# Retention, ELU and max-out in one kernel: the loads and the order of its first eight chunks

## The chip, the cores and the metric

The kernel runs on one core of a Trainium2 chip. The metric is the device time of one execution in microseconds (us), the median over several executions. TensorE (PE in the profile) multiplies matrices, VectorE (DVE), ScalarE (ACT) and GpSimd (POOL) work elementwise, and SyncE (SP) issues most of the DMAs.

## What is computed

The reference has three layers over 4 batches of 768 tokens (3072 rows of 512).

```
state = gamma * state + outer(k_t, v_t)          # 8 heads of 64, per batch
y_t   = scale * q_t @ state
x     = y as 3072 x 512
h     = x @ w_in;  g = h if h > 0 else exp(h) - 1
x2    = g @ w_out                                 # 512 -> 2048 -> 512
h2    = max(x2 @ w1, x2 @ w2, x2 @ w3)            # 512 -> 768
out   = h2 @ moe2_w_out                           # 768 -> 512
```

The weights of the second and third layer come as 64-bit floats and are converted on the chip to a high and a low 32-bit part.

## The kernel before

**Chunks.** The recurrence is taken in 24 chunks of 128 tokens, six to a batch. A chunk `c` is one SBUF tile `x` of 128 partitions by 4 head pairs by 4 slots of 128: slot 0 is q and slot 1 is k, both with the head dimension on the partitions (first head of a pair on partitions 0 to 63, second on 64 to 127), slots 2 and 3 are k and v by token. The first eight chunks (`early`, `EARLY` = 8) read from `qkv0`, whose row of 640 floats holds two blocks of 128 for q (the first head's in the first, for partitions 0 to 63; the second head's in the second, for partitions 64 to 127), then k, k by token and v by token, 128 each. The others read from `qkv`.

**Work of a chunk.** `load` (lines 78 to 109) issues its DMAs on SP. `prep` (113 to 143) multiplies q by the decays `qdec_sb` into `qd` (line 130; left out for the first chunk of a batch) and k by token by `cols_sb` into `kd` (line 136, eight ScalarE instructions; left out for the last chunk of a batch). `scores` (145 to 154) multiplies k and q on TensorE, `mask` (156 to 169) multiplies the two results by the constants `dmask_sb` on VectorE. `mix` (194 to 217) multiplies the old state by `qd` (line 205) and the values by the masked scores (209), and ScalarE copies the sum to `xh`, the high part of the layer's input; `update` (173 to 192) makes the new state; `rest` (219) makes the low part `xl`. `begin` (531) is `scores`, `prep`, `mask`; `finish` (540) is `mix` with `update` between its matmuls and its copy. `junk(k)` (526) runs k matmuls on zeros.

**Weights.** `load_half(n)` (234) loads a half tile of weights, 512 KB in rows of 4096 bytes, into one of two staging buffers (`raw`); `cv_bits`, `cv_rest`, `cv_high` and `cv_low` (274 to 309) convert it on VectorE and ScalarE; `cv_high(n)` issues the load of half n + 2, into the buffer that half n leaves. Halves 0 and 1 serve the first `h1` and `o1` (331 and 359, the two matmul groups of the second layer, 12 matmuls of 128x512 each), halves 2 and 3 the next.

**Order.** SP, PE, DVE and ACT each run in the order in which the program text names their instructions. Each waits at its own next instruction, and nothing overtakes. The first part is written out by hand (lines 500 to 600); after it a loop runs `h1` and `o1` over blocks of 512 tokens. SP's order in the first part: chunks 0, 1, 2, half 0, chunk 3, half 1, chunks 4 to 7, then half 2, which `cv_high(0)` issues. An early chunk takes four DMAs: q of the first heads (line 98, 64 partitions, 128 KB), q of the second heads (98, 64 partitions, 128 KB), k (100, 128 partitions, 256 KB), k and v by token (106, 128 partitions, 512 KB). Each contiguous run is 512 bytes in the first three and 1024 bytes in the last. The constants `cols`, `dmask` (512 KB) and `qdec` (256 KB) are issued from ScalarE's queue. From chunk 8 on a chunk takes four DMAs of 64 partitions (98, runs of 512 bytes) and one of 128 partitions (106).

Of the kernel before, what the change touches and what calls it, by code (L numbers as in the profile page):

```python
# [15 lines left out]
B, H, S, D = 4, 8, 768, 64  # L16
P = 128
# [23 lines left out]
def kernel(ctx: ExitStack, tc: tile.TileContext, qkv0, qkv, wa, wb, dmask, qdec, cols, out):  # L41


    nc = tc.nc
# [6 lines left out]
    ps_acc = ctx.enter_context(tc.tile_pool(name="ps_acc", bufs=4, space=bass.MemoryType.PSUM))  # L51
# [9 lines left out]
    dmask_sb = const.tile([P, H, P], F32, name="dmask_sb")  # L61
    qdec_sb = const.tile([P, NPAIR, P], F32, name="qdec_sb")
# [7 lines left out]
    def f32(ap):  # L70
        return ap.bitcast(F32)
# [6 lines left out]
    def load(c, part=None):  # L78


        if c >= NCHUNK:
            return

        early = c < EARLY
        src = qkv0 if early else qkv
        if part != 1:
            if c in raw_t:
                return
            if c < EARLY + 3:
                x = wpool.tile([P, NPAIR, 4, P], F32, tag="w", name="x")  # L90
            else:
                x = ld.tile([P, NPAIR, 4, P], F32, tag="r", name="x")
            raw_t[c] = x
            for r in range(2):
                h = slice(r * D, (r + 1) * D)
                for s in range(1 if early else 2):
                    cc = slice(s * 2 * P + r * P, s * 2 * P + (r + 1) * P)
                    nc.sync.dma_start(out=x[h, :, s, :], in_=src[c, :, h, cc].rearrange("p d t -> d p t"))
            if early:
                nc.sync.dma_start(  # L100
                    out=x[:, :, 1, :], in_=src[c, :, :, 2 * P:3 * P].rearrange("p t n -> t p n")
                )
        if part != 0:
            x = raw_t[c]
            o = 3 * P if early else 4 * P
            nc.sync.dma_start(
                out=x[:, :, 2:4, :].rearrange("t p s n -> t p (s n)"),
                in_=src[c, :, :, o:].rearrange("p t n -> t p n"),
            )
# [3 lines left out]
    def prep(c):  # L113

        if c >= NCHUNK:
            return
        x = raw_t[c]
        early = c < EARLY
        pool = nc.vector if early else nc.gpsimd
        if c < EARLY + CB and c % 2:  # L120
            if c in (1, EARLY + 1):
                spare[:] = [wpool.tile([P, 4, NPAIR, P], F32, tag="w", name="spare")]
            sp = spare[0]
            qd, kd, a = sp[:, 0], sp[:, 1].rearrange("t p (r d) -> t p r d", r=2), sp[:, 2:4]
        else:
            qd = at.tile([P, NPAIR, P], F32, tag="qd", name="qd") if c % NCH != 0 else None
            kd = at.tile([P, NPAIR, 2, D], F32, tag="kd", name="kd") if c % NCH != NCH - 1 else None
            a = None
        if c % NCH != 0:
            pool.tensor_tensor(out=qd, in0=x[:, :, 0, :], in1=qdec_sb, op=ALU.mult)  # L130
        kt = x[:, :, 2, :].rearrange("t p (r d) -> t p r d", r=2)
        if c % NCH == NCH - 1:
            pass
        elif early:
            for h in range(H):
                nc.scalar.activation(kd[:, h // 2, h % 2], kt[:, h // 2, h % 2], ACTF.Copy, scale=cols_sb[:, h:h + 1])
        else:
            pool.tensor_tensor(
                out=kd, in0=kt,
                in1=cols_sb[:, 0:H].rearrange("t (p r) -> t p r", r=2).unsqueeze(3).to_broadcast([P, NPAIR, 2, D]),  # L140
                op=ALU.mult,
            )
        st_t[c] = (qd, kd, a)

    def scores(c, pool, tag):

        if c >= NCHUNK:
            return
        x = raw_t[c]
        sc = sc_t[c] = [pool.tile([P, NPAIR, P], F32, tag=tag, name="sc") for _ in range(2)]  # L150
        for p in range(NPAIR):
            for r in range(2):
                h = slice(r * D, (r + 1) * D)
                nc.tensor.matmul(sc[r][:, p, :], x[h, p, 1, :], x[h, p, 0, :], start=p == 0, stop=p == NPAIR - 1)  # L154

    def mask(c):
        if c >= NCHUNK:
            return
        sc = sc_t.pop(c)
        a = st_t[c][2]  # L160
        if a is None:
            a = at.tile([P, 2, NPAIR, P], F32, tag="a", name="a")
        else:
            a = a.rearrange("t r p i -> t r p i")
        for r in range(2):
            nc.vector.tensor_tensor(
                out=a[:, r], in0=sc[r], in1=dmask_sb.rearrange("j (p r) i -> j r p i", r=2)[:, r], op=ALU.mult
            )
        a_t[c] = a
# [49 lines left out]
    def rest(c):  # L219
        b, t0 = divmod(c * P, BLK)  # L220
        xh, xl = x_t[b]
        nc.vector.tensor_tensor(
            out=xl[:, :, t0:t0 + P], in0=xo_t.pop(c), in1=f32(xh[:, :, t0:t0 + P]), op=ALU.subtract
        )
# [49 lines left out]
    def cv_bits(n):  # L274
        if n >= len(keys):
            return
        t = dpool.tile([P, 512], I32, tag="t", name="t")
        m = dpool.tile([P, 512], F32, tag="m", name="m")
        tmp[n] = (t, m)
        nc.vector.tensor_scalar(  # L280
            out=t, in0=half[n][:, :, 1], scalar1=0x7FFFFE00, scalar2=None, op0=ALU.bitwise_and
        )
        nc.scalar.activation(t, t, ACTF.Relu, scale=8.0, bias=-896.0 * 2 ** 23)  # L283

    def cv_rest(n):
        if n >= len(keys):
            return
        m = tmp[n][1]
        lo, hi = half[n][:, :, 0].bitcast(U32), half[n][:, :, 1]
        nc.vector.tensor_scalar(out=m.bitcast(I32), in0=hi, scalar1=0x1FF, scalar2=None, op0=ALU.bitwise_and)  # L290
        nc.vector.scalar_tensor_tensor(  # L291
            out=m, in0=lo, scalar=2.0 ** -32, in1=m.bitcast(I32), op0=ALU.mult, op1=ALU.add
        )

    def cv_high(n):
        to[n] = place(n)
        t = tmp[n][0]
        nc.vector.scalar_tensor_tensor(  # L298
            out=t, in0=half[n][:, :, 1], scalar=-0x80000000, in1=t, op0=ALU.bitwise_and, op1=ALU.bitwise_or
        )  # L300
        nc.scalar.copy(to[n][:, 0], f32(t))  # L301
        load_half(n + NSTAGE)
# [200 lines left out]
    warm = dpool.tile([P, 1], F32, tag="m", name="warm")  # L503
    nc.vector.memset(warm, 0.0)
    nc.scalar.dma_start(out=cols_sb, in_=cols)
    nc.scalar.dma_start(out=dmask_sb, in_=dmask)
    nc.scalar.activation(warm, warm, ACTF.Exp)
    nc.scalar.dma_start(out=qdec_sb, in_=qdec)
    load(0)
    load(1)  # L510
    load(2)
    load_half(0)
    load(3)
# [12 lines left out]
    def junk(k):  # L526
        o = ps_h.tile([P, BLK], F32, tag="h", name="junk")
        for i in range(k):
            nc.tensor.matmul(o, zero[:, 0:P], zero, start=i == 0, stop=i == k - 1)

    def begin(c, pool=ps_h, tag="h"):
        scores(c, pool, tag)
        prep(c)
        mask(c)
# [5 lines left out]
    def finish(c):  # L540
        mix(c, ps_h, "h", update)
# [5 lines left out]
    finish(0)  # L547
    rest(0)
    junk(4)
    begin(2, ps_acc, "acc")  # L550
    finish(1)
    rest(1)
    cv_bits(0)
    begin(3, ps_acc, "acc")
    finish(2)
    rest(2)
    cv_rest(0)
    cv_high(0)
    finish(3)
# [4 lines left out]
    begin(4, ps_h, "h")  # L564
    h1(0, 0, [(cv_high, 1)])
    prep(5)
    finish(4)
    cv_low(1)
    scores(5, ps_h, "h")
    mask(5)  # L570
    rest(4)
    prep(6)
    o1(0, 0, 0, 2)
    cv_bits(2)
# [25 lines left out]
    n = 5  # L600
# [178 lines left out]
    for i, (b, f, f0, f1) in enumerate(seq):  # L779
# [8 lines left out]
        c = EARLY  # L788
# [94 lines left out]
    for v, (s, j) in enumerate(visits):  # L883
# [3 lines left out]
        if 2 <= v < 2 + KF2:  # L887
            f = v - 2
            t = ring.tile([P, 2, 512], F32R, tag=f"w{f % 2}", name="w")
# [87 lines left out]
```

## Time and profile before

| | us |
|---|---|
| median of 3 executions (1004.82 to 1005.65) | 1004.98 |
| the profiled execution | 1005.29 |
| its span, first to last instruction | 1003.5 |
| PE busy | 984.8 (98%) |
| DVE busy | 690.7 (69%) |
| ACT busy | 352.9 (35%) |
| POOL busy | 35.9 (4%) |

Busy time is that of instructions of the engine; waits and the issuing of DMAs don't count. PE's is modelled from pipelined matmuls and counts junk matmuls too. The granted TensorE clock is 1.000 of full speed over the whole span. In the DMA columns a share over 1 means that packets overlap in an engine.

### The profile page before, as it was taken

Reading aid. Unit: us, or ns where it says so; the run is one execution under the profiler, and the core shown is the slowest. Engines: PE = TensorE matmul, PEld = TensorE weight load, DVE = VectorE, ACT = ScalarE, POOL = GpSimd, SP = SyncE. Lnnn points to the kernel's source line nnn. Section 1 sums busy time; section 2 is a strip of 40 time slices with the busy share of each in tenths; the row PEclk is TensorE's granted clock in tenths of the full one; section 3 lists DMA queues with packets and bytes.
Section 4 is the critical chain, followed back from the end, with each engine's and each line's share of the span. In section 5 each row is a group of like instructions: output and inputs, shape, how many; then the busy total and the mean of one; then the engine's idle time right before and its main releaser. Section 6 shows DMA issues by size and latency. Waiting matters only on the chain.

```text
span 1003.5 us, 14377 instructions
## 1 busy us (share of the span) xinstructions
PE 984.8 (98%) x5684; PEld 848.0 (85%) x5685; DVE 690.7 (69%) x1190; ACT 352.9 (35%) x630; POOL 35.9 (4%) x31
## 2 busy tenths in 40 slices
PE   7989999999999999999999999999999999999998
PEld 5777888777888888888888788999899989989996
DVE  4889989975576776677776743688658827864771
ACT  4546555422434444444434443311301311130110
POOL 0000000120011100001100000000000000000000
PEclk9999999999999999999999999999999999999999
DMA  9723336876538773696428717983355055204601
GB/s 272 202 83 106 104 127 198 277 218 207 179 98 268 262 256 96 230 314 211 157 85 325 282 54 271 373 322 145 105 177 212 1 185 211 98 22 156 253 1 63
DMA packets 75315, 180.78 MB, mean 180 GB/s; under 512 B 5872, under 2 KB 42736, under 8 KB 71024
## 3 DMA queue, kind: packets, MB, share of 16 engines
q1 hardware_dynamic: 73088, 175.92, 51.6%
q10 hardware_dynamic: 2160, 3.94, 1.1%
q8 instruction: 45, 0.74, 0.3%
q14 instruction: 22, 0.18, 0.1%
HBM read 139.20 MB, written 40.63 MB: 179 GB/s over the span
## 4 chain that ended last, share of the span: by engine, by line
PE 86%; DVE 7%; DMA 4%; ACT 2%; issue 1%; SPq 0%; ACTq 0%; DVEq 0%
PE pp L693 26%; PE hp L339 24%; PE acc L371 23%; PE ac L745 10%; DMA x<-in_qkv 2%; DMA raw<-in_wa 1%; PE xo L209 1%; PE sc L154 1%; PE xo L205 1%; DVE gl L352 1%; DVE e L348 1%; DVE part L388 1%; DVE t L298 1%; ACT gh L349 1%; DVE w L307 1%; DVE m L291 1%
## 5 line engine op out<-in xcount | busy, mean ns | idle before, releaser
L693 PE MATMUL pp<-xs,op 128*128 128x384 f32 x1512 | 267.8, 334 | 0.0
L693 PEld LDWEIGHTS pp<-xs,op 128*128 128x128 f32 x1512 | 263.3, 188 | 3.0
L339 PE MATMUL hp<-xh,w 128*128 128x512 f32 x768 | 248.1, 394 | 4.7 <-DVE state L192 2.5
L371 PE MATMUL acc<-gh,w 128*128 128x512 f32 x768 | 193.9, 391 | 3.1 <-ACT w L301 1.7
L339 PEld LDWEIGHTS hp<-xh,w 128*128 128x128 f32 x768 | 143.7, 188 | 38.1 <-ACT w L301 2.4
L371 PEld LDWEIGHTS acc<-gh,w 128*128 128x128 f32 x768 | 143.0, 188 | 36.4 <-ACT w L301 2.6
L348 DVE SCALAR_TENSOR_TENSOR e<-e,hp 128x512 f32<-128x512 f32 x96 | 65.7, 685 | 111.6 <-ACT e L347 111.6
L339 PE MATMUL hp<-xl,w 128*128 128x512 f32 x384 | 141.9, 390 | 0.0
L745 PE MATMUL ac<-w,g 128*128 128x512 f32 x432 | 104.5, 391 | 0.0
L371 PE MATMUL acc<-gl,w 128*128 128x512 f32 x384 | 102.7, 389 | 0.0
L346 ACT ACTIVATE e<-hp 128x512 f32<-128x512 f32 x96 | 57.2, 596 | 103.0 <-PE hp L339 102.9
L745 PEld LDWEIGHTS ac<-w,g 128*128 128x128 f32 x432 | 80.6, 188 | 14.9
L349 ACT CAST gh<-e 128x512 fp32r<-128x512 f32 x96 | 59.7, 622 | 89.0 <-DVE e L348 89.0
L709 ACT COPY u<-pp 128x384 f32<-128x384 f32 x36 | 17.3, 480 | 201.2 <-PE pp L693 140.9
L371 PEld LDWEIGHTS acc<-gl,w 128*128 128x128 f32 x384 | 72.1, 188 | 15.1
L339 PEld LDWEIGHTS hp<-xl,w 128*128 128x128 f32 x384 | 72.1, 188 | 14.4
L352 DVE TENSOR_TENSOR gl<-e,gh 128x512 fp32r<-128x512 f32 x96 | 68.5, 713 | 19.7 <-ACT gh L349 16.9
L701 DVE TENSOR_TENSOR c<-pp,u 128x384 f32<-128x384 f32 x96 | 52.8, 553 | 36.1 <-PE pp L693 35.7
L347 ACT ACTIVATE e<-e 128x512 f32<-128x512 f32 x96 | 60.7, 633 | 3.1
L283 ACT ACTIVATE t<-t 128x512 int32<-128x512 int32 x56 | 35.4, 633 | 54.1 <-DVE t L280 54.1
L301 ACT CAST w<-t 128x512 fp32r<-128x512 f32 x56 | 34.8, 621 | 43.4 <-DVE t L298 40.0
L723 DVE TENSOR_TENSOR h<-h,c 128x768 f32<-128x768 f32 x48 | 45.9, 957 | 1.6
(72 smaller groups left out, 817.1 us busy)
## 6 DMA issues: line engine op xcount, KB each, us to landing
op<-opd SPq DMA_DIRECT2D x24, 1792.0 KB, 7.5
w<-kept SPq DMA_DIRECT2D x56, 512.0 KB, 6.7
raw<-in_wa SPq DMA_DIRECT2D x32, 512.0 KB, 3.7
x<-in_qkv SPq DMA_DIRECT2D x24, 512.0 KB, 6.2
raw<-in_wb SPq DMA_DIRECT2D x24, 512.0 KB, 4.4
x<-in_qkv SPq DMA_DIRECT2D x80, 128.0 KB, 5.3
opd<-w SPq DMA_DIRECT2D x9, 1024.0 KB, 8.0
kept<-w SPq DMA_DIRECT2D x14, 512.0 KB, 5.6
```

Source lines behind the costliest of these rows:

```text
L283: nc.scalar.activation(t, t, ACTF.Relu, scale=8.0, bias=-896.0 * 2 ** 23)
L339: nc.tensor.matmul(hp, w[:, pw, kk * P:(kk + 1) * P], x[px][:, kk, :], start=k == 0, stop=k == len(order) - 1,)
L346: nc.scalar.activation(e, hp, ACTF.Exp)
L347: nc.scalar.activation(e, e, ACTF.Relu, scale=-1.0, bias=1.0)
L348: nc.vector.scalar_tensor_tensor(out=e, in0=e, scalar=-1.0, in1=hp, op0=ALU.mult, op1=ALU.max)
L349: nc.scalar.copy(gh, e)
L352: nc.vector.tensor_tensor(out=gl, in0=e, in1=f32(gh), op=ALU.subtract)
L371: nc.tensor.matmul(acc_t[b][m], w[:, p[0], m * P:(m + 1) * P], g[p[1]], start=f == f0 and p == first, stop=f == f1 - 1 and p == final,)
L693: nc.tensor.matmul(o, ws[i][:, pw, kk * P:(kk + 1) * P], xs[i][:, px, kk, :], start=k == 0, stop=k == 5)
L701: nc.vector.tensor_tensor(out=out, in0=a, in1=c, op=ALU.add)
L723: nc.vector.tensor_tensor(out=h_t[s, p][i], in0=h_t[s, p][i], in1=c[i], op=ALU.max)
L745: nc.tensor.matmul(ac_t[s, m], g[:, px, m * P:(m + 1) * P], wo_t[f][:, pw, :], start=first and i == 0, stop=final and i == 2,)
```

## The change

The early chunks are loaded by DMAs of 64 partitions each. Chunks 0 and 1 come in two parts: part 0 is q of the first heads (runs of 512 bytes), k of the first heads (512) and q and k of the second heads in one (1024); part 1 is, as before, k and v by token (128 partitions, 1024). Chunks 2 to 7 come in three DMAs: q of the first heads (128 KB, runs of 512 bytes), all four slots of the second heads (512 KB, 2048), and the other three slots of the first heads (384 KB, 1536). The bytes are the same. `dmask` and `qdec` go from ScalarE's queue to SP's, `dmask` behind part 0 of chunk 0 and `qdec` behind part 0 of chunk 1. `qd` of an early chunk is made on GpSimd and no more on VectorE. `begin(2)` now follows `finish(1)` and `rest(1)`, `begin(3)` follows `finish(2)` and `rest(2)`, and there is one more `junk(4)`.

```diff
@@ -91,15 +91,28 @@
             else:
                 x = ld.tile([P, NPAIR, 4, P], F32, tag="r", name="x")
             raw_t[c] = x
-            for r in range(2):
-                h = slice(r * D, (r + 1) * D)
-                for s in range(1 if early else 2):
-                    cc = slice(s * 2 * P + r * P, s * 2 * P + (r + 1) * P)
-                    nc.sync.dma_start(out=x[h, :, s, :], in_=src[c, :, h, cc].rearrange("p d t -> d p t"))
             if early:
-                nc.sync.dma_start(
-                    out=x[:, :, 1, :], in_=src[c, :, :, 2 * P:3 * P].rearrange("p t n -> t p n")
-                )
+                last = 2 if part == 0 else 4
+
+                def slots(h, s0, s1, c0):
+                    nc.sync.dma_start(
+                        out=x[h, :, s0:s1, :].rearrange("d p s n -> d p (s n)"),
+                        in_=src[c, :, h, c0:c0 + (s1 - s0) * P].rearrange("p d t -> d p t"),
+                    )
+
+                slots(slice(0, D), 0, 1, 0)
+                if part == 0:
+                    slots(slice(0, D), 1, last, 2 * P)
+                slots(slice(D, P), 0, last, P)
+                if part is None:
+                    slots(slice(0, D), 1, last, 2 * P)
+                    return
+            else:
+                for r in range(2):
+                    h = slice(r * D, (r + 1) * D)
+                    for s in range(2):
+                        cc = slice(s * 2 * P + r * P, s * 2 * P + (r + 1) * P)
+                        nc.sync.dma_start(out=x[h, :, s, :], in_=src[c, :, h, cc].rearrange("p d t -> d p t"))
         if part != 0:
             x = raw_t[c]
             o = 3 * P if early else 4 * P
@@ -116,7 +129,7 @@
             return
         x = raw_t[c]
         early = c < EARLY
-        pool = nc.vector if early else nc.gpsimd
+        pool = nc.gpsimd
         if c < EARLY + CB and c % 2:
             if c in (1, EARLY + 1):
                 spare[:] = [wpool.tile([P, 4, NPAIR, P], F32, tag="w", name="spare")]
@@ -503,11 +516,13 @@
     warm = dpool.tile([P, 1], F32, tag="m", name="warm")
     nc.vector.memset(warm, 0.0)
     nc.scalar.dma_start(out=cols_sb, in_=cols)
-    nc.scalar.dma_start(out=dmask_sb, in_=dmask)
     nc.scalar.activation(warm, warm, ACTF.Exp)
-    nc.scalar.dma_start(out=qdec_sb, in_=qdec)
-    load(0)
-    load(1)
+    load(0, 0)
+    nc.sync.dma_start(out=dmask_sb, in_=dmask)
+    load(0, 1)
+    load(1, 0)
+    nc.sync.dma_start(out=qdec_sb, in_=qdec)
+    load(1, 1)
     load(2)
     load_half(0)
     load(3)
@@ -547,13 +562,14 @@
     finish(0)
     rest(0)
     junk(4)
-    begin(2, ps_acc, "acc")
     finish(1)
     rest(1)
+    begin(2, ps_acc, "acc")
     cv_bits(0)
-    begin(3, ps_acc, "acc")
+    junk(4)
     finish(2)
     rest(2)
+    begin(3, ps_acc, "acc")
     cv_rest(0)
     cv_high(0)
     finish(3)
```

## Rows read from the trace of the kernel before

**Rows 1.** Page: busy time of each engine, share of the span, instructions.
```profile
PE 984.8 (98%) x5684; PEld 848.0 (85%) x5685; DVE 690.7 (69%) x1190; ACT 352.9 (35%) x630; POOL 35.9 (4%) x31
```

**Rows 2.** Stretches: PE, PEld, DVE, ACT, POOL busy (instructions), PEclk, DMA share, GB/s.
```profile
0.00:50.00 50.00, 41.96 (x476) 31.00 (x479) 31.16 (x58) 25.58 (x76) 0.20 (x4) 1.00 0.88 238
50.00:100.00 50.00, 46.82 (x246) 37.88 (x243) 44.44 (x84) 28.26 (x49) 0.00 (x0) 1.00 0.28 95
100.00:150.00 50.00, 50.00 (x222) 41.41 (x221) 44.85 (x82) 28.07 (x46) 0.00 (x0) 1.00 0.36 116
```

**Rows 3.** The chain of waits, first 80 us, pieces in order: start, us, what.
```profile
14.15 8.86 DMA x<-in_qkv
...
34.25 7.28 DMA raw<-in_wa
...
41.55 0.43 DVE t L280
...
44.35 3.03 PE hp L339 x12
```

**Rows 4.** PE's longest waits from 80 us on: us in total, times, longest.
```profile
PE hp L339 <- DVE state L192: 2.5, 3, 1.4
PE acc L371 <- ACT t L283: 0.9, 1, 0.9
```

**Rows 5.** Timeline of SP: chunk 1's last DMA, and halves 2 and 3.
```profile
6.47 0.82 SPq L106 DMA_DIRECT2D x<-in_qkv  x1
...
34.25 1.98 SPq L244 DMA_DIRECT2D raw<-in_wa  x2
```

**Rows 6.** Landing of chunk 1's last DMA: KB, us from issue.
```profile
x<-in_qkv SPq DMA_DIRECT2D x1, 512.0 KB, 7.2
```

**Rows 7.** Short stretches, columns as in Rows 2: chunks 1 and 2, then chunk 12 on.
```profile
11.75:12.25 0.50, 0.48 (x7) 0.39 (x8) 0.02 (x1) 0.46 (x2) 0.00 (x0) 1.00 1.11 342
13.40:14.40 1.00, 1.00 (x28) 0.97 (x24) 0.94 (x2) 0.70 (x3) 0.00 (x0) 1.00 1.19 260
314.00:315.00 1.00, 1.00 (x6) 0.82 (x5) 1.00 (x2) 0.00 (x0) 0.00 (x0) 1.00 1.22 211
416.00:417.00 1.00, 1.00 (x6) 0.84 (x5) 0.79 (x2) 0.00 (x0) 0.00 (x0) 1.00 1.22 220
```

**Rows 8.** DMA packets in 189.75:191 (a half of weights) and in 415.6:417.4.
```profile
DMA packets 133, 0.50 MB, mean 397 GB/s; under 512 B 16, under 2 KB 16, under 8 KB 131
...
DMA packets 743, 0.39 MB, mean 219 GB/s; under 512 B 43, under 2 KB 743, under 8 KB 743
```

**Rows 9.** Timeline of SP around the last rows' stretch: a late chunk's four half-tile DMAs.
```profile
411.06 2.58 SPq L98 DMA_DIRECT2D x<-in_qkv  x4
```

**Rows 10.** Timeline of PE: first scores; fourth chunk's layer; the wait for half 2.
```profile
8.41 1.16 PE L154 MATMUL sc<-x 64*128 64x128 f32 x16 [2.22 <-DMA x<-in_qkv]
...
29.16 1.19 PE L339 MATMUL hp<-xh,w 128*128 128x512 f32 x4 [0.47 <-ACT xh L217]
...
44.35 1.19 PE L339 MATMUL hp<-xh,w 128*128 128x512 f32 x4 [1.35 <-ACT w L301]
```

**Rows 11.** Timeline of DVE: from chunk 3's low part to the wait for half 2.
```profile
25.61 0.69 DVE L222 TENSOR_TENSOR xl<-xo,xh 128x512 fp32r<-128x512 f32 x1 [0.64 <-ACT xh L217]
...
41.55 0.43 DVE L280 TENSOR_SCALAR t<-raw 128x512 int32<-128x512 int32 x1 [1.16 <-DMA raw<-in_wa]
```

**Rows 12.** Line 130 (`qd`) on DVE and POOL: ns min/median/max, first and last start.
```profile
L130 POOL TENSOR_TENSOR qd<-x,qdec_sb x12: 1270/1377/1707, 177.9 to 509.9; 128x512 f32<-128x512 f32 x12
...
L130 DVE TENSOR_TENSOR spare<-x,qdec_sb x4: 682/684/691, 11.1 to 45.4; 128x512 f32<-128x512 f32 x4
```

**Rows 13.** Timelines of POOL and of DVE at 178 us.
```profile
177.94 1.29 POOL L130 TENSOR_TENSOR qd<-x,qdec_sb 128x512 f32<-128x512 f32 x1 [177.49 <-DMA x<-in_qkv]
...
178.00 1.78 DVE L298 SCALAR_TENSOR_TENSOR t<-raw,t 128x512 int32<-128x512 int32 x1
```

## The prediction, made before the changed kernel ran

> **What bounds the kernel now.** I read the busy times first, then stretches, the chain of waits, the short stretches by DMA rate, and last the engines' own timelines. TensorE is busy for 98% of the span at the full clock [rows 1], so nothing short of less or earlier TensorE work moves the end. The stretches show where it is not full: 8 of its 19 idle us lie in the first 50, 3 in the next 50, and from 100 to 150 there is none [rows 2]. After 80 us its two longest waits sum to 3.4 us [rows 4], all on engines and none on a load. So a delay or a gain made before about 80 us reaches the end one to one, and the question is what sets the pace before.
>
> In the first 50 us the DMA engines are busy for 0.88, against 0.28 in the next 50 [rows 2]. The chain says which transfer ends that phase: half 2 of the weights, issued at 34.25 and landed at 41.53 [rows 3]. VectorE has waited 1.16 us for it [rows 11] and TensorE 1.35 us for what is made of it [rows 10]. Behind it stands only conversion and matmul work, no load. Half 2 is the last of the queue: 512 KB behind all eight chunks. So the time at which SP's queue has drained sets the time of everything later, and the change is first of all a change of that drain.
>
> **The loads, chunks 2 to 7.** Between the landing of chunk 1 (6.47 + 7.2 = 13.67 [rows 5, 6]) and that of half 2 (41.53) lie six chunks of 1.049 MB and three halves of 0.524 MB: 27.86 us. A half goes at 397 GB/s [rows 8], 1.32 us; three are 3.96. That leaves 23.9 us, 3.98 us a chunk.
>
> The new chunk is the same bytes in three DMAs, each on 64 partitions only. The trace has no such DMA with long runs; it bounds the rate from both sides. With long runs on all 128 partitions: 342 GB/s for runs of 1024 bytes [rows 7], 397 for 4096 [rows 8]; at 397 for the 0.918 MB in long runs and 260 for the 0.131 MB in short ones a chunk takes 2.31 + 0.50 = 2.8 us. With 64 partitions and runs of 512: the late chunks issue four such DMAs in a row, and while they pass the engines are busy (share 1.22) and move 211 to 220 GB/s [rows 7], 219 over 1.8 us [rows 8]. SP had issued them by 413.64 [rows 9], so at 416 the issue doesn't limit them. At 211 a chunk takes 4.97 us. That it isn't the run of 512 alone shows in the early chunks: there short runs on 64 and on 128 partitions alternate, at about the same run, and pass at 260 [rows 7]. Partition count costs something by itself. I take 217, the middle of the 64-partition rows, since partitions are what the new DMAs share with them and run length is what they don't: 1.049 MB / 217 = 4.83 us a chunk, 0.85 more than now, 5.1 us over six chunks.
>
> [...]
>
> **The loads, chunks 0 and 1.** Part 0 is 0.524 MB on half the partitions: 2.42 us at 217, against 2.02 at 260 now; part 1 stays. Two chunks cost 0.8 us. Against it, `dmask` and `qdec` now leave on one queue behind the first queries and share nothing with them: the first scores, at 8.41 after 2.22 us of waiting [rows 10], may come up to 2 us sooner. The queue carries the same bytes up to chunk 1, so its drain gains nothing by that; a smoother start may take back some of the 0.8. I take +0.4, with 0 and 0.8 as ends. The sum for half 2 is +5.5: landing at 47.0.
>
> **The order of PE.** Scores of chunks 2 and 3 wait for all of a chunk, q to v; behind `finish` of the chunk before, that wait holds up nothing that is ready. Without the new order it would hold `mix(1)` and `mix(2)`. The cost of the order is nothing, since the loads are later than both. The extra `junk(4)` (some 1 us) lies in the wait for chunk 3. Chunk 4 does hold something: `scores(4)` stand before the first `h1` on PE. Chunk 4 lands at 13.67 + 0.4 + 3 x 4.83 + 2 x 1.32 = 31.2, so `h1`, at 29.16 now [rows 10], starts after 32.3, 3.2 us later. That is less than half 2's 5.5 and is hidden behind it: VectorE, which runs without a break from 25.61 to 40.4 [rows 11], then reaches half 2 at about 43.5 and waits for 47.0.
>
> **Decays on GpSimd.** Six multiplications leave VectorE (0.68 us each [rows 12], about 0.6 from start to start) and take 1.27 to 1.71 on GpSimd. Between 25 and 40 us, where VectorE is full, two are saved, 1.2 us; but one beside a GpSimd instruction took 1.78 us in place of 0.68 [rows 13], so each can also cost 1.1 where they meet. From -0.6 to +0.5 a piece, all ahead of the wait for half 2, except the last (chunk 7), where `scores(7)` are waited for: I take 0 and keep -0.6 to +0.5. If the loads didn't bind, 1.2 us would come off the end.
>
> **Sum.** The profiled execution took 1005.29, of which the span is 1003.5; with +5.5 it is 1010.8. The median shown is 0.3 below the profiled one, so the forecast is **1010.5**. Its own range: chunks at 225 and no loss at the start give +4.1 - 0.6 (1008.5), at 211 with 0.8 and 0.5 give +7.2 (1012.2).
>
> **Rivals.**
> *The run length decides, and the kernel is faster.* For it: 512-byte runs pass at 260, 1024 at 342, 4096 at 397 [rows 7, 8], and the change halves the runs' number. Against it: the late 64-partition rows. Place: the same drain; it decides from 260 GB/s up, where 1.049 MB take 4.03 us, about what they take now. At 342 a chunk takes 3.07, and half 2 would land at 13.67 + 6 x 3.07 + 3.96 = 36.0. VectorE then sets the pace: it starts its full stretch when chunk 3 is in, 14.15 + 8.86 = 23.0 now [rows 3], and 13.67 + 2 x 3.07 + 1.32 = 21.1 then, 1.9 sooner; with 1.2 us of decays gone too it is ready for half 2 at 40.4 - 3.1 = 37.3 and begins there, in place of 41.55 [rows 11]. That is 4.2, with chunk 7's decay up to 4.8; 4.6 gives **1000.4**.
>
> *The halves overlap.* First-head and second-head DMAs lie behind each other in the queue; if engines are far enough apart, both halves' rates add up and the mean is the 260 of the early rows. Then 4.03 against 3.98 a chunk: +0.3, less up to 0.6 for chunk 7's decay: **1004.8**, no change. For it: 260 was measured while 64-partition DMAs of both halves and k alternated. Against it: there a DMA was 128 KB, here 512 and 384, so that most of each passes with its own half alone. [...]
>
> [...]
>
> **Chances.** Forecast 0.58, lower clock on top 0.11, overlap 0.11, run length 0.20. A measurement of this kernel can tell 0.2%, 2.0 us, from no change. Slower by more: 0.58 + 0.11 = 0.69; within: 0.11; faster: 0.20. The range reaches from 1000.0 to 1013.5: half of the run-length case lies below it, half of the clock case above. The likeliest case alone has 1008.5 to 1012.2.
>
> **What would show it.** Right: in the stretches from 15 to 45 us a DMA share over 1 at 205 to 230 GB/s; half 2 of the weights in the chain, landing at 46 to 48; VectorE idle for 3 us or so ahead of line 280; the second `h1` at 49 to 51; nothing changed after 80 us but the shift. First scores at 6.3 to 7.5. Wrong: 300 GB/s or more in those stretches, and half 2 landing before 38; or half 2 late and VectorE not waiting, which would mean that the decays' or the scores' new order holds up the engines themselves; or a shift that shrinks after 80 us.

## The result, and the profile after

The changed kernel takes 1014.41 us (median of 4, 1013.63 to 1016.69), the kernel before, run beside it, 1005.32 (1004.82 to 1005.86): a ratio of 1.0097 with a 95% interval of 1.0085 to 1.0110, slower by 9.1 us. The forecast was 1010.5 with a range up to 1013.5. The profiled execution took 1013.63, its span 1011.9, 8.4 more than before.

TensorE is busy for 5.0 us more and idle for 3.4 more [rows 1]; busy time here holds the twelve matmuls that take 4.63 us in place of 3.03 (below, at a lower granted clock) and the added `junk(4)`, 1.04, too, so it takes the chain to say what is late:

```profile
PE 989.8 (98%) x5689; PEld 851.7 (84%) x5689; DVE 689.8 (68%) x1184; ACT 353.1 (35%) x630; POOL 43.5 (4%) x37
```

The chain of waits of the changed kernel, first 60 us, answers to [rows 3] (start, us, what):

```profile
3.47 6.66 DMA x<-in_qkv
...
35.95 13.98 DMA raw<-in_wa
49.96 0.43 DVE t L293
...
52.76 4.63 PE hp L352 x12
```

The same half 2 of the weights still ends the load phase, but lands at 49.93, 8.4 later, and the twelve matmuls behind it take 4.63 us in place of 3.03. On the engines' timelines the wait for it is 4.58 us on VectorE and 4.31 on TensorE (1.16 and 1.35 before [rows 10, 11]). Two rows of VectorE after the change:

```profile
44.70 0.68 DVE L235 TENSOR_TENSOR xl<-xo,xh 128x512 fp32r<-128x512 f32 x1
49.96 0.43 DVE L293 TENSOR_SCALAR t<-raw 128x512 int32<-128x512 int32 x1 [4.58 <-DMA raw<-in_wa]
```

And four of TensorE: the first scores, the mix of chunk 1, the second `h1` and the first matmuls of the next group:

```profile
6.82 1.16 PE L167 MATMUL sc<-x 64*128 64x128 f32 x16
...
20.78 1.09 PE L218 MATMUL xo<-spare,state 64*64 64x128 f32 x16 [3.14 <-POOL spare L143]
...
52.76 1.39 PE L352 MATMUL hp<-xh,w 128*128 128x512 f32 x4 [4.31 <-ACT w L314]
...
65.61 1.21 PE L384 MATMUL acc<-gh,w 128*128 128x512 f32 x4 [1.36 <-ACT w L314]
```

The second `h1` starts 8.4 later than in [rows 10], its successor at 65.61, 10.0 later than the 55.59 of before. The difference, 1.6 us, is the slower `h1`. Stretches after the change, columns as in Rows 2; the first two lie where the loads run, the next five are the end of the queue, the last two the second `h1`:

```profile
20.50:24.00 3.50, 3.22 (x60) 2.99 (x62) 0.57 (x2) 1.06 (x4) 0.22 (x1) 1.00 1.08 233
36.50:40.50 4.00, 3.29 (x36) 2.35 (x38) 3.96 (x6) 2.65 (x9) 0.97 (x1) 1.00 1.10 227
...
46.00:47.00 1.00, 1.00 (x21) 0.83 (x18) 0.00 (x0) 0.00 (x0) 0.52 (x1) 1.00 1.01 222
47.00:48.00 1.00, 1.00 (x20) 0.83 (x17) 0.00 (x0) 0.00 (x0) 0.75 (x1) 1.00 0.98 385
48.00:48.50 0.50, 0.45 (x9) 0.26 (x6) 0.00 (x0) 0.00 (x0) 0.00 (x0) 1.00 0.79 262
48.50:49.00 0.50, 0.00 (x0) 0.00 (x0) 0.00 (x0) 0.00 (x0) 0.00 (x0) 1.00 0.17 66
49.50:50.00 0.50, 0.00 (x0) 0.00 (x0) 0.04 (x1) 0.00 (x0) 0.00 (x0) 1.00 0.06 25
...
50.00:55.00 5.00, 2.24 (x7) 1.80 (x8) 4.85 (x9) 3.65 (x11) 0.00 (x0) 0.86 0.34 102
55.00:60.00 5.00, 4.83 (x49) 3.73 (x49) 0.78 (x2) 1.79 (x3) 0.00 (x0) 0.80 0.03 10
```

The engines are busy (share over 1) and move 222 to 233 GB/s up to 47.0; then the rate jumps to 385. Not all that passes slowly is chunks. A row of weights is a packet of 4096 bytes, and the runs of chunk 7's last DMA have 1536. Of the 96 packets from 45.5 to 47 us, 73 have 2 to 8 KB, and they are rows of weights, since chunk 7's runs of 2048 bytes landed at 45.1:

```profile
DMA packets 96, 0.33 MB, mean 223 GB/s; under 512 B 10, under 2 KB 22, under 8 KB 95
```

So half 2, with its 128 partitions, begins while the last rows of chunk 7 still pass, and at first at no more than the rate of the half-tile DMAs. Half 2 is not the last of the queue, as the prediction has it: half 3, issued at 40.92, follows in the same stretches (from 47 to 48.5 another 122 such packets pass, some 0.50 MB or 4.1 KB each, and a half has 128), so 385 is not the rate of half 2 alone. From 48.5 on almost nothing moves, yet half 2 is not in before 49.93: what is left hangs on a few DMA engines (share 0.17 from 48.5 to 49, 0.06 from 49.5 to 50). And the granted clock, 1.00 throughout before, is 0.86 and 0.80 behind TensorE's wait.

The start of the queue is late too. SP's row of chunk 1's last DMA and its landing, answering [rows 5, 6]: 6.71 + 8.3 = 15.0, where it was 13.67.

```profile
6.71 0.43 SPq L119 DMA_DIRECT2D x<-in_qkv  x1
```

```profile
x<-in_qkv SPq DMA_DIRECT2D x1, 512.0 KB, 8.3
```

Later the loss shrinks. PE's longest waits from 80 us on, after the change:

```profile
PE hp L352 <- DVE state L205: 2.3, 3, 1.3
PE acc L384 <- ACT gh L362: 0.5, 1, 0.5
```

The wait of 0.9 us for line 283 [rows 4], which stood at 197 us, is gone: what TensorE waited for there was not late with it. Of the 10.0 us at 65.61 8.4 reach the end.

### The profile page after: what moved, and what is told of

Same layout as the page of the kernel before. It is cut to its first block, busy times and chain, and to the rows that moved or that the text cites. A ratio compares the mean times of both kernels' runs of the same rounds, so it can differ in the third digit from the quotient of the medians.

```text
span 1011.9 us, 14384 instructions
## 1 busy us (share of the span) xinstructions
PE 989.8 (98%) x5689; PEld 851.7 (84%) x5689; DVE 689.8 (68%) x1184; ACT 353.1 (35%) x630; POOL 43.5 (4%) x37
## 4 chain that ended last, share of the span: by engine, by line
PE 86%; DVE 6%; DMA 6%; ACT 1%; issue 0%; SPq 0%; DVEq 0%
PE pp L709 26%; PE hp L352 24%; PE acc L384 22%; PE ac L761 10%; DMA raw<-in_wa 4%; DMA x<-in_qkv 2%; PE xo L222 1%; PE sc L167 1%; PE xo L218 1%; DVE gl L365 1%; DVE e L361 1%; DVE part L401 1%; DVE t L311 1%; DVE m L304 1%; ACT gh L362 0%; DVE w L320 0%
## 5 line engine op out<-in xcount | busy, mean ns | idle before, releaser
L314 ACT CAST w<-t 128x512 fp32r<-128x512 f32 x56 | 34.8, 621 | 44.9 <-DVE t L311 41.5
```

## Experiments

Times are medians; ratios are to the kernel before on the same chip, with 95% intervals.

**1. The loads alone, and all but the loads.** `loads_only` is the kernel before with the new `load` (first fragment); `rest_only` is the changed kernel with the old one (second), so with its constants, order, decays and `junk(4)`.

```diff
-    load(0)
-    load(1)
+    load(0, 0)
+    load(0, 1)
+    load(1, 0)
+    load(1, 1)
```

```diff
-                slots(slice(0, D), 0, 1, 0)
...
+            for r in range(2):
+                h = slice(r * D, (r + 1) * D)
...
+            if early:
+                nc.sync.dma_start(
+                    out=x[:, :, 1, :], in_=src[c, :, :, 2 * P:3 * P].rearrange("p t n -> t p n")
+                )
```

> The kernel before with the new load shape of the first eight chunks alone; constants on ScalarE's queue, order of PE and decays on VectorE as before. Theory (DMAs on one half of the partitions move at 215 to 230 GB/s, and the drain of the queue sets the rest): half 2 of the weights lands at 47 to 50 us, time 1011.5 to 1015.5, at least four fifths of the change's 9.1 us. Rival (constants on one queue, the new order or GpSimd carry half of the loss): 1009 to 1010.

> The changed kernel with the loads as they were before; constants on SP's queue, new order of PE, decays on GpSimd stay. Theory: the drain is the old one, half 2 lands at 41 to 43 us, time 1004 to 1007. Rival: mix of chunk 1 waits for its decays on GpSimd (3.1 us in the changed kernel), and that alone costs 3 to 5 us: 1008 to 1010, with half 2 on time.

Measured: `loads_only` 1014.86, ratio 1.0094 (1.0077 to 1.0111); `rest_only` 1007.26, 1.0018 (1.0006 to 1.0031). The loads by themselves lose as much as the whole change. With them half 2 lands at 50.17, just behind the expected 47 to 50 (chain of waits of `loads_only`):

```profile
37.14 13.03 DMA raw<-in_wa
...
52.99 5.47 PE hp L352 x12
```

`rest_only` comes out just above its 1004 to 1007. In its profile, the slowest of its ten executions, half 2 lands at 45.2 in place of 41 to 43, and the mix of chunk 1 waits 3.35 us for GpSimd; behind that wait the granted clock is down to 0.50:

```profile
20.00:23.00 3.00, 3.00 (x36) 2.81 (x35) 0.03 (x1) 0.90 (x3) 1.19 (x1) 0.50 1.08 328
```

**2. Partitions or run length.** Four kernels, all the changed kernel with another cut of chunks 2 to 7. `whole`, `halves` and `middle` read four consecutive blocks on all partitions, in runs of 2048 bytes, on 0 to 127 at once, on 0 to 63 and 64 to 127, and on 32 to 95, 0 to 31 and 96 to 127. The line with the bounds differs between them. They leave out q of the first heads in these chunks, since the four blocks read begin behind it; a chunk has the same number of bytes. `short` keeps the changed kernel's halves, but one slot, a run of 512 bytes, in each DMA.

```diff
+                if part is None:
+                    for lo, hi in ((32, 96), (0, 32), (96, 128)):
+                        slots(slice(lo, hi), 0, 4, P)
+                    return
```

> The changed kernel, but chunks 2 to 7 come in one DMA of 128 partitions with runs of 2048 bytes, the same 1.049 MB a chunk. It leaves out q of the first heads in these chunks: zeros of the input stand in their place. Theory (the half of the partitions is what is slow): 380 GB/s or so, 2.8 us a chunk, half 2 lands at 35 to 38, time 1000 to 1003. Rival (long runs out of these rows, or the one queue, are what is slow): 215 to 235 GB/s as in the changed kernel, 1012 to 1015.

> As whole, with the DMA cut in two, partitions 0 to 63 and 64 to 127, runs of 2048 bytes, the same bytes. Theory: 215 to 235 GB/s, 4.5 to 4.9 us a chunk, half 2 at 47 to 50, 1012 to 1015. Rival (what is slow is the short DMA of 128 KB or the uneven cut 128, 512, 384 KB): 300 GB/s or more, 1001 to 1005.

> As whole, cut in three: partitions 32 to 95, then 0 to 31, then 96 to 127, runs of 2048 bytes, the same bytes. [...] If what counts is how many partitions a DMA has, 64 and 32 are no better than 64 and 64: 4.8 us or more a chunk, 1013 or more.

> The changed kernel with the 512 and 384 KB DMAs of chunks 2 to 7 cut by slots, so that every run is 512 bytes on 64 partitions, eight DMAs a chunk; nothing is left out. Theory (a half's limit holds whatever the run): 210 to 225 GB/s, 0 to 2 us slower than the changed kernel, 1014 to 1016.5. Rival (the longer runs buy something on a half too): 1018 or more.

Measured: `whole` 1004.23, 0.9993 (0.9980 to 1.0005); `halves` 1015.24, 1.0101 (1.0051 to 1.0152); `middle` 1010.71, 1.0053 (1.0018 to 1.0088); `short` 1017.76, 1.0126 (1.0097 to 1.0156). `halves` and `short` ran twice each. DMA packets from 16 to 32 us, first `whole`, then `halves`, with some rows of weights in both:

```profile
DMA packets 2893, 6.24 MB, mean 390 GB/s; under 512 B 111, under 2 KB 111, under 8 KB 2891
```

```profile
DMA packets 1479, 3.36 MB, mean 210 GB/s; under 512 B 104, under 2 KB 104, under 8 KB 1478
```

The same runs of 2048 bytes pass at 390 on all partitions and at 210 on halves. Stretches of `middle`, as in Rows 2; in the first and third mostly 32 to 95 pass, in the second the two outer quarters and behind them a half of the weights, in the fourth the outer quarters:

```profile
13.00:14.50 1.50, 1.50 (x29) 1.38 (x26) 1.08 (x2) 0.00 (x0) 0.00 (x0) 1.00 1.09 379
15.00:18.00 3.00, 0.99 (x7) 0.31 (x4) 1.37 (x3) 2.02 (x8) 0.00 (x0) 1.00 1.07 258
18.50:20.00 1.50, 0.00 (x0) 0.00 (x0) 0.00 (x0) 0.00 (x0) 1.33 (x2) 0.50 1.10 395
20.00:21.00 1.00, 0.00 (x0) 0.00 (x0) 0.00 (x0) 0.00 (x0) 1.00 (x1) 0.50 1.05 238
```

So it is not the count of 64 that halves the rate, but which 64: partitions 32 to 95 pass at 379 to 395, as fast as all 128 (390 in `whole`), where the halves 0 to 63 and 64 to 127 pass at 210. What in the chip makes the two kinds of 64 differ these runs don't show.

What run length does on a half these runs don't settle. From 33 to 43 us chunks alone pass; the stretch in `halves`, in the changed kernel and in `short`, and SP's row of `short`:

```profile
33.00:43.00 10.00, 8.48 (x120) 6.94 (x116) 8.16 (x13) 5.06 (x17) 2.92 (x2) 1.00 1.07 224
33.00:43.00 10.00, 9.19 (x95) 7.12 (x96) 9.31 (x18) 7.01 (x18) 1.45 (x1) 1.00 1.09 226
33.00:43.00 10.00, 8.48 (x82) 7.13 (x84) 5.74 (x11) 4.67 (x14) 1.87 (x2) 0.83 0.80 203
```

```profile
24.75 23.61 SPq L98 DMA_DIRECT2D x<-in_qkv  x32
```

Runs of 2048 bytes and the changed kernel's of 512 to 2048 go at the same rate. `short` is slower by 3.4 us than the change, but there the engines are not full (share 0.80): SP takes 0.74 us for each of its 32 DMAs, 5.9 for the eight of a chunk, which is more than the 4.8 that a chunk takes in the changed kernel. Its loss can be SP's issuing as well as the runs.

The times of `whole`, `halves` and `short` lie outside their theories' ranges. `whole` has its loads as expected (half 2 at 35.5), but not the gain. `halves` has half 2 at 52.5, later than its 47 to 50. `middle`, at 1010.71, lies below the 1013 expected if the count of partitions decides. Its half 2 lands at 44.4, and VectorE doesn't wait for it, but the mix of chunk 1 waits 5.16 us for GpSimd, and the granted clock falls to 0.50 in that wait (the third and fourth row).

**3. The clock.** `warm` is the changed kernel with 14 junk matmuls ahead of the second `h1`, where TensorE waits.

```diff
     mask(6)
+    junk(14)
     h1(0, 1, [], [(cv_bits, 3)])
```

> The changed kernel with 14 junk matmuls (some 3.2 us) ahead of the second first-layer group, in TensorE's gap of 4.3 us. Theory (the gap lowers the granted clock, and that costs the 1.6 us by which those 12 matmuls take 4.63 in place of 3.03): granted clock 1.00 in 50 to 60 us, 1012.5 to 1013.5. Rival (the clock falls for another reason, or what it costs is hidden): 1014 to 1015.

Measured: 1012.21, ratio 1.0073 (1.0056 to 1.0090), 2.2 us below the changed kernel, with intervals that just overlap. Stretch 50 to 60 us of `warm` at a granted clock of 1.00, the chain's row of the twelve matmuls, and VectorE's of half 2:

```profile
50.00:60.00 10.00, 8.85 (x86) 6.57 (x85) 6.91 (x13) 5.98 (x16) 0.00 (x0) 1.00 0.15 54
```

```profile
52.26 2.76 PE hp L352 x12
```

```profile
48.92 0.43 DVE L293 TENSOR_SCALAR t<-raw 128x512 int32<-128x512 int32 x1 [2.50 <-DMA raw<-in_wa]
```

The slower `h1` is the clock: with it kept at 1.00 the matmuls take 2.76 us in place of 4.63, 1.9 less. The next group starts 2.4 us sooner, at 63.23; the other 0.5 comes from half 2, which with the same loads landed 1.0 sooner in this profile. The loads still cost the rest.

**4. Weight halves ahead of the chunks.** `early_halves` is the changed kernel with halves 0 and 1 issued ahead of chunk 2, so that only half 2 stands behind half-tile DMAs.

```diff
-    load(2)
     load_half(0)
-    load(3)
     load_half(1)
+    load(2)
+    load(3)
```

> The changed kernel, with halves 0 and 1 of the weights issued ahead of chunk 2 in place of behind chunks 2 and 3, so that they pass behind 128-partition DMAs only. Theory (a weight half that stands behind a half-partition DMA is itself slowed, to about 1.9 us in place of 1.33, because some DMA engines reach it while others still carry the half-partition rows): halves 0 and 1 pass at 330 to 400 GB/s, half 2 lands at 48.5 to 49.3 in place of 49.93, and the time is 0.5 to 1.5 us below the changed kernel, less what chunks 2 and 3 lose by coming 2.7 us later. Rival (all 7.86 MB behind chunk 1 pass at the one rate of the half, whatever their order): half 2 lands within 0.4 us of 49.93.

Measured: 1013.10, ratio 1.0078 (1.0065 to 1.0091), 1.3 us below the changed kernel, with half 2 in at 49.0 (issued 37.90, 11.1 to landing). Stretches of it: one in the two halves, then most of the six chunks:

```profile
14.40:15.40 1.00, 1.00 (x10) 1.00 (x12) 0.87 (x2) 0.61 (x3) 0.00 (x0) 0.50 1.01 406
...
16.00:32.00 16.00, 9.99 (x124) 7.79 (x122) 4.33 (x9) 4.40 (x15) 4.42 (x4) 0.75 1.10 219
32.00:46.00 14.00, 12.75 (x178) 10.43 (x174) 12.16 (x21) 8.71 (x25) 2.01 (x2) 1.00 1.10 218
```

Apart, the two kinds go at 406 and at 218 to 219. Half 2 lands in the theory's range, 0.9 us sooner than in the changed kernel; but 0.3 of that was there when chunk 1 landed (14.8 against 15.0), and in `warm`, which has the changed kernel's order, it landed at 48.9 too. So these profiles don't show that the order of the halves is worth anything. The time is no clean measure of it either: here the second `h1` waits for VectorE and no longer for the load, and the low clock stands elsewhere (0.75 from 16 to 32 us, where the mix of chunk 1 waits 6.0 us).

**5. The other parts one by one.** `const_only` and `pool_only` are the kernel before with one edit each, the constants' queue and the decays' engine.

```diff
-    nc.scalar.dma_start(out=dmask_sb, in_=dmask)
...
+    load(0, 0)
+    nc.sync.dma_start(out=dmask_sb, in_=dmask)
+    load(0, 1)
+    load(1, 0)
+    nc.sync.dma_start(out=qdec_sb, in_=qdec)
+    load(1, 1)
```

```diff
-        pool = nc.vector if early else nc.gpsimd
+        pool = nc.gpsimd
```

> The kernel before, with one edit: the mask constants and the query decays leave on SP's queue, the mask behind the first two DMAs (q of both heads) and k of chunk 0, the decays behind those of chunk 1, in place of ScalarE's queue. Loads, order and decays are as before. Theory (the change's loss is all in the half-partition loads; the constants only reorder the same bytes ahead of chunk 1): first scores 1 to 2 us sooner than 8.41, chunk 1's landing within 0.5 us of 13.67, half 2 at 41.0 to 42.0, time within 2 us of before. Rival (first scores set the pace of everything behind them, so this part is worth a gain of its own): half 2 is reached ready and the time falls by 1 us or more.

> The kernel before, with one edit: the query decays of the first eight chunks are made on GpSimd in place of VectorE. Theory (VectorE's saving and what a neighbouring GpSimd instruction costs it cancel; but GpSimd takes chunk 2's decay ahead of chunk 1's, which holds chunk 1's mix by 2 to 4 us as it did with the old loads and the new order): TensorE's first matmul of line 205 waits 2 to 4 us for GpSimd's second decay, the first h1 comes 1 to 3 us later than 29.16, and the time rises by 1 to 3 us, which would be the whole of what the change without its loads costs (1007.26 against 1005.4). Rival (the new order costs it): no such wait, time within 1 us of before.

Measured: `const_only` 1006.32, 1.0016 (1.0002 to 1.0029); `pool_only` 1005.93, 1.0009 (1.0001 to 1.0018). With the constants on SP the first scores come at 7.14 in place of 8.41, but half 2 at 42.10 in place of 41.53, and nothing is won. The loss of `const_only` goes with the clock: its five executions at a mean granted clock of 1.000 took 1003.92 to 1005.75, the seven at 0.995 to 0.999 took 1005.54 to 1010.79. Its profile is one of the five and doesn't show what lowers the clock in the others. GpSimd and the row of TensorE that waits for it, in `pool_only`:

```profile
15.72 1.27 POOL L130 TENSOR_TENSOR qd<-x,qdec_sb 128x512 f32<-128x512 f32 x1 [15.28 <-DMA x<-in_qkv]
16.95 1.27 POOL L130 TENSOR_TENSOR spare<-x,qdec_sb 128x512 f32<-128x512 f32 x1
```

```profile
18.27 1.09 PE L205 MATMUL xo<-spare,state 64*64 64x128 f32 x16 [0.59 <-POOL spare L130]
```

GpSimd takes chunk 2's decay (`qd`) ahead of chunk 1's (`spare`), though chunk 1 is in first (the kernel fixes the order of its text for SP, PE, DVE and ACT, not for GpSimd); the first waits for chunk 2's load, the second for the first. The expected wait of 2 to 4 us is 0.59 here, since the old order has `scores(2)` in the same place, waiting for the same load; with the new order it is open, 3.35 us in `rest_only` and 3.14 in the changed kernel. The first `h1` starts at 31.27, 2.1 later, and the second at 46.58, 2.2 later, of which the time shows 0.8 to 0.9 and the span of this profile 1.1. By the times that is within the rival's 1 us. Both edits lose a little by themselves; that the two of them make up the 1.9 of `rest_only` fits, but the intervals are too wide to prove it.

**6. A version with wide, long runs.** `tall_k` is the kernel before with chunks 2 to 7 in three DMAs: q of both halves as before, and k with k and v by token in one of 128 partitions (runs of 1536 bytes). `tall_order` has the change's order of scores in addition.

```diff
+            if early and c > 1:
+                nc.sync.dma_start(
+                    out=x[:, :, 1:4, :].rearrange("t p s n -> t p (s n)"),
+                    in_=src[c, :, :, 2 * P:].rearrange("p t n -> t p n"),
+                )
+                return
```

> The kernel before; in chunks 2 to 7 k, k by token and v by token come in one DMA of 128 partitions with runs of 1536 bytes, in place of two (512 and 1024); q in its two halves of 128 KB as before. Theory (partitions decide first, then run length): 0.786 MB at about 380 GB/s take 2.1 us and q 1.1, a chunk 3.2 in place of 3.8; half 2 lands at 38 to 39.5, time 1002 to 1004. Rival (run length does nothing, or scores that now wait for k with the values take it back): 1005 to 1007.

> The kernel before, with chunks 2 to 7 in three DMAs (q of each half of the heads as before; k, k by token and v by token in one of 128 partitions, runs of 1536 bytes), and scores of chunks 2 and 3 behind the mix of the chunk before, as in the change; constants and decays as before, no added junk matmuls. Theory (with wide, long runs the loads no longer end last; what then held the front was the scores of chunk 2, waiting 1.65 us ahead of a mix that was ready): that wait lies behind the mix, the first h1 starts at 29 to 30 in place of 31.03, and the time is 1.5 to 3 us below before, 1002 to 1003.5. Rival (the front is bound by the sum of TensorE's and VectorE's own work, so that the order only moves the wait): within 1 us of before.

Measured: 1004.53, 0.9991 (0.9981 to 1.0000), and 1004.60, 0.9993 (0.9985 to 1.0002). In neither does the second `h1` wait for a load any more, and in `tall_order` the scores of chunk 2 hold up nothing; but the second `h1` starts at 44.98 and at 43.60, against 44.35 before. Both miss their forecast of time, and half 2 lands at 41.1 in `tall_k`, not at 38 to 39.5. The plainest case is `whole`: its half 2 lands at 35.5, 6 us sooner than before, and its second `h1` starts at 43.89. So the front is bound by the engines' own work within a microsecond of where the loads bind it now, and no cut of these loads tried here is worth more than 1 us by its median (2 us by its interval).

## Why the prediction was right and where it failed

**Right: the mechanism.** A half of the partitions passes at little over one half of the rate at the same runs (210 GB/s in `halves` against 390 in `whole`), and the drain of SP's queue sets what follows. "1.049 MB / 217 = 4.83 us a chunk" holds: by the rows of `early_halves` at 218 to 219 it is 4.80. First scores were to come at 6.3 to 7.5 and come at 6.82. VectorE waits for half 2, for 4.58 us where about 3 were expected.

**Failed: "The sum for half 2 is +5.5".** It was +8.4. From chunk 1's landing (6.71 + 8.3 = 15.0) on, the same 7.86 MB took 34.93 us in place of 27.86, +7.07 where the sum has +5.1. The step that fails is "A half goes at 397 GB/s, 1.32 us; three are 3.96", used for both kernels. Landings of the last DMA of each chunk and half, in SP's order (issue plus time to landing, as for chunk 1):

| us | chunk 1 | 2 | half 0 | 3 | half 1 | 4 | 5 | 6 | 7 | half 2 |
|---|---|---|---|---|---|---|---|---|---|---|
| before | 13.7 | 17.1 | 18.6 | 23.0 | 25.0 | 29.1 | 33.0 | 37.1 | 40.3 | 41.5 |
| after | 15.0 | 19.9 | 21.7 | 26.6 | 28.4 | 32.9 | 37.7 | 42.4 | 47.4 | 49.9 |

From landing to landing the three halves take 4.8 us before and 6.2 after, not 3.96 in both; the six chunks take 23.1 and 28.7.
- The old chunk is therefore 3.85, where 3.98 was taken, and the new one 4.79, close to the forecast 4.83. Chunks cost some 5.6 and not 5.1.
- The halves cost 1.4, where the sum has nothing. Most of it is half 2, which lands 2.5 behind chunk 7 where it landed 1.3 behind it; its first rows pass at no more than the rate of the half-tile DMAs (223 GB/s from 45.5 to 47), and its last hang on a few engines (share 0.17 and less), as shown above.
- The split is not firm. The packets of neighbours overlap, and other profiles of the same loads differ: from chunk 1 to half 2 `loads_only` and `warm` take 34.4 in place of 34.9, with 6.0 and 5.2 for the halves. For the loads as before, `const_only` and `pool_only` have 28.1 and 28.0, but `rest_only` 30.3, which stays open.

Chunks 0 and 1 took 1.33 more, against the 0.4 of the sum and its ends of 0 and 0.8. What of that is the half-tile DMAs is open: chunk 1 lands at 13.94 in `const_only` (6.34 + 7.6) and at 14.94 in `rest_only` (6.34 + 8.6), two kernels with the same loads.

**The lower clock had a chance of 0.11 and came true at half its price.** Its case stands at 1013.5, 3.0 above the forecast; that 3.0 was the author's assumption and no run shows it. The changed kernel showed 1.6: the twelve matmuls of the second `h1` took 4.63 us in place of 3.03, at a mean granted clock of 0.63:

```profile
52.76:57.39 4.63, 4.63 (x14) 3.35 (x16) 2.30 (x4) 1.87 (x8) 0.00 (x0) 0.63 0.37 113
```

TensorE's gap ahead of them was 4.31 us, with half 2 in 3 us later than forecast. Behind a wait of 3.35 in `rest_only` the clock fell too, to 0.50. The four times of the changed kernel follow the mean granted clock of their executions: 0.997 for 1013.63, 0.995 for 1013.75 and 1015.08, 0.993 for 1016.69.

**"So a delay or a gain made before about 80 us reaches the end one to one" was too strong.** The prediction itself named a shift that shrinks after 80 us as a sign of being wrong. 10.0 us at 65.61 became 8.4 at the end, and in `pool_only` 2.2 at the second `h1` became 1.1 in the span. Of the 1.6 lost on the way, 0.9 is the vanished wait for line 283 [rows 4]; where the remaining 0.7 went was not settled.

**"The cost of the order is nothing" and decays at 0** hold in the total only because the loads are later. `rest_only` costs 1.9: the prediction counted GpSimd's durations and its cost to VectorE (below), not that GpSimd would take chunk 2's decay first and hold up the mix of chunk 1, nor the clock behind that wait. The 1.9 was not split among them. The first `h1`, "after 32.3", starts at 34.26.

**The rivals.** Run length as the cause is refuted on halves by `halves` (210 to 224 at 2048 bytes). Its time of 1000.4 was too good in any case: `whole` reaches 390 GB/s and gains 0.6 us, within its interval of nothing. Overlapping halves are refuted: in `halves` the DMAs of both sides stand in turn in the queue, and together they move 210 to 224, not the 260 that this rival needs.

From the forecast to the median: +2.9 for half 2, +1.6 for the clock, -1.6 recovered, and +1.1 because the median now lies 0.8 above the profiled execution where 0.3 below was taken: 4.0, which is the 3.9 that it missed by but for rounding.

## What to carry to other kernels

Before merging DMAs for longer runs, look at which partitions each one still touches: here the late chunks' rows on the same 64 partitions gave 217 GB/s for the forecast, the new DMAs moved 218 to 219 in `early_halves`, and runs of 2048 bytes did not repair it (210 to 224 in `halves`). When a queue is slowed, price everything in it by rows from beside such transfers, the wide transfers between them and the last one's tail too. And a wait that grows on TensorE can have two prices, its own length and the clock of what follows: here 4.31 us of it, with 1.6 more for twelve matmuls at 0.63 behind it.

## What the runs showed of the chip beyond that

- One DMA on partitions 32 to 95 moved 379 to 395 GB/s, those on 0 to 63 or 64 to 127 211 to 233.
- A 128-partition transfer right behind half-partition ones did not pass at 397 GB/s: from 45.5 to 47 us mostly its rows passed, at 223, and in its last 1.4 us 66 GB/s and less moved.
- After TensorE waits of 4.27 to 4.31 us the granted clock was 0.65 to 0.86 in the next 5 us stretches (50 to 60 us of `loads_only` and the changed kernel), and twelve matmuls of 128x512 took 4.63 to 5.47 us in place of 3.03. Behind a wait of 3.35 it was 0.50 in `rest_only`, behind one of 3.14 it was 1.00 in the changed kernel. But there it fell to 0.77 between 10 and 15 us as well, where the waits of TensorE were only 1.05 and 0.66 us, while before a wait of 2.22 [rows 10] left it at 1.00; why was not tried.
- Three VectorE operations beside a GpSimd one took 1.42 to 1.76 us; the same three lines took 0.41, 0.69 and 0.42 without one. From its timeline in the changed kernel:

```profile
18.19 1.42 DVE L202 TENSOR_TENSOR state<-state,cols_sb 128x256 f32<-128x256 f32 x1
...
31.32 1.76 DVE L311 SCALAR_TENSOR_TENSOR t<-raw,t 128x512 int32<-128x512 int32 x1
...
36.25 1.51 DVE L303 TENSOR_SCALAR m<-raw 128x512 int32<-128x512 int32 x1
```
